# Windowed attention and a squared-ReLU MLP on one core: from the framework's order of work to an order written by a list scheduler

## The chip, the core and the metric

The kernel runs on 1 core of one Trainium2 chip. The metric is the device time of one execution in microseconds (us). The core's engines are TensorE (PE in the profile; its weight loads are PEld), VectorE (DVE), ScalarE (ACT), GpSimd (POOL) and SyncE (SP). TensorE writes its results to PSUM, 8 banks of 2 KB in each of 128 partitions, from where VectorE or ScalarE copy them to SBUF. DMAs are issued from SyncE's queue (by hardware descriptors) or GpSimd's (by software descriptors, which can also cast on the way).

## The reference

For 4 batches of 8 heads, 768 tokens, head size 64: attention in which a query sees the last 128 keys and the first 4 ("sinks"). Its output, 3072 tokens of 512, goes through two layers with a squared ReLU between them.

```python
scores = scale * np.matmul(q, k.transpose(0, 1, 3, 2))
keep = (pos[None, :] < 4) | ((rel >= 0) & (rel < 128))     # rel = query - key
a = softmax(np.where(keep, scores, -1e9))
x = np.matmul(a, v)                 # then heads side by side: (3072, 512)
h = x @ w_in                        # (512, 2048)
r = np.maximum(h, 0.0)
return (r * r) @ w_out              # (2048, 512), float32
```

Inputs and output are float32.

## The kernel before

All matmuls are in bf16. Work is tiled by 128 tokens (6 tiles, NT, to a batch) and by pairs of heads (4, NP, to a batch).

*Loads* (`load_qk_dma` line 112, `load_v` line 140, `load_w_in_dma` line 89, `load_w_out_dma` line 94): all from GpSimd's queue, cast from float32 to bf16 on the way. A head of q, k or v is one DMA of 768 rows of 64 elements. w_in is four DMAs, w_out four.

*Transposes* (`load_qk_compute`, line 124): for each head pair and each of q and k six 128x128 TensorE transposes into one PSUM tile (line 131), and one VectorE copy to `qkT` (line 138), in which the two heads of a pair lie on partitions 0 to 63 and 64 to 127.

*Attention* (line 150), head pair by head pair: scores of 64-row matmuls into two one-bank PSUM buffers (lines 171, 178), keys on the partitions, each block of 128 keys against the 256 queries that can see it; exp on ScalarE (line 185). The sinks are taken as a whole first key block of 128 against queries 256 to 767 (line 191), and a bias of -100 in the exponential (line 197) clears the rows beyond the fourth. A mask multiply on VectorE (line 203), then 15 matmuls per head with v, which carries a column of ones, so that column 64 is the softmax sum (line 224, one PSUM buffer); a reciprocal and a multiply on VectorE (lines 232, 233) write `xn`.

*Bridge* (line 240): for each token tile four transposes and a copy to `xT_sb`.

*Layer 1* (`moe1`, line 258): for each of 16 blocks of 128 hidden columns, 4 matmuls on 512 tokens and 4 on 256 (line 265), into two one-bank PSUM buffers; ReLU on ScalarE (line 272) and the square in place on VectorE (line 273). *Layer 2* (`moe2`, line 275): for each token tile 16 matmuls of 512 columns (line 281), a copy on VectorE (line 288), and the store from SyncE (line 289).

The order: the calls at the end of the kernel (lines 291 to 324) give attention of batches 0 and 1, then layer 1 and 2 of a batch followed by attention of the next but one. The framework's own scheduler reorders the instructions of these calls by readiness and priority within the buffer counts of the pools (lines 45 to 58); in the trace layer 1 of one batch runs mixed with attention of the next.

## Time and profile before

| | |
|---|---|
| time, median of 3 runs | 288.06 us (287.36 to 288.46) |
| span of the profiled execution, first to last instruction | 285.6 us |
| TensorE busy | 256.0 us, 90% |
| VectorE, ScalarE, GpSimd busy | 133.0, 125.3, 89.8 us |
| granted TensorE clock, mean | 0.998 |
| DMA packets | 81429, of which 77952 on GpSimd's software queue |

Times are microseconds, unless a column says ns. In a time table by stage each row is a stretch of the span, with the busy time of each engine and its number of instructions in brackets, then the granted clock, the DMA engines' busy share and GB/s. In the chain of waits and the timeline a row has start, length and what ran. In a list of groups a row has line, engine, operation, output and input tile with shapes, count, then busy us, mean ns of one, and the idle time before them with what ended it. In the list of DMA queues a row has packets, MB, and the packets' time as a share of 16 engines' span. A matmul's length holds its latency; matmuls overlap, so a burst is shorter than the sum of its parts.

### The profile page before, as it was taken

Reading aid. Unit: us, or ns where it says so; the run is one execution under the profiler, and the core shown is the slowest. Engines: PE = TensorE matmul, PEld = TensorE weight load, DVE = VectorE, ACT = ScalarE, POOL = GpSimd, SP = SyncE. Lnnn points to the kernel's source line nnn. Section 1 sums busy time; section 2 is a strip of 40 time slices with the busy share of each in tenths; the row PEclk is TensorE's granted clock in tenths of the full one; section 3 lists DMA queues with packets and bytes.
Section 4 is the critical chain, followed back from the end, with each engine's and each line's share of the span. In section 5 each row is a group of like instructions: output and inputs, shape, how many; then the busy total and the mean of one; then the engine's idle time right before and its main releaser. Section 6 shows DMA issues by size and latency. Waiting matters only on the chain.

```text
span 285.6 us, 4652 instructions
## 1 busy us (share of the span) xinstructions
PE 256.0 (90%) x1859; PEld 135.5 (47%) x1888; DVE 133.0 (47%) x307; ACT 125.3 (44%) x257; POOL 89.8 (31%) x127
## 2 busy tenths in 40 slices
PE   1586775999999999999999999999999999999994
PEld 0333444564555444555555445644554444555441
DVE  2343554587674212785863114776753113333211
ACT  1175540489945100798754001899553003455000
POOL 8999679775996000970000000000000000000000
PEclk9999999999999999999999999999999999999999
DMA  8979999999999012990000111000000221000121
GB/s 57 120 52 163 210 158 127 145 157 170 126 109 110 37 73 76 135 122 3 2 1 2 73 73 73 3 2 0 2 0 0 85 85 52 2 1 0 73 76 73
DMA packets 81429, 20.23 MB, mean 71 GB/s; under 512 B 75776, under 2 KB 77824, under 8 KB 81408
## 3 DMA queue, kind: packets, MB, share of 16 engines
q0 software_dynamic: 77952, 13.64, 61.1%
q1 hardware_dynamic: 3456, 6.29, 6.0%
q8 instruction: 15, 0.25, 0.4%
q14 instruction: 6, 0.05, 0.1%
HBM read 27.26 MB, written 6.29 MB: 117 GB/s over the span
## 4 chain that ended last, share of the span: by engine, by line
PE 74%; ACT 8%; DVE 6%; POOL 6%; issue 2%; DMA 2%; POOLq 0%
PE pm L281 28%; PE pm L265 27%; PE po L224 6%; POOL qn L117 5%; ACT expm L185 4%; PE ps L171 4%; PE pxt L246 3%; ACT gT L272 3%; DVE expm L203 3%; PE pt L131 2%; PE ps L191 2%; DMA v_aug<-in_v_dram 2%; PE ps L178 2%; DVE qkT L138 1%; DVE xn L233 1%
## 5 line engine op out<-in xcount | busy, mean ns | idle before, releaser
L272 ACT ACTIVATE gT<-pm 128x512 bf16<-128x512 f32 (+1 forms) x128 | 59.1, 490 | 109.2 <-PE pm L265 108.5
L265 PE MATMUL pm<-xT_sb,w_in_sb 128*128 128x256 bf16 (+1 forms) x498 | 102.6, 326 | 3.6 <-ACT gT L272 1.7
L281 PE MATMUL pm<-w_out_sb,gT 128*128 128x512 bf16 x369 | 85.2, 379 | 0.4
L265 PEld LDWEIGHTS <-w_in_sb 128*128 128x128 bf16 x512 | 46.0, 98 | 40.1 <-issue 19.7
L185 ACT ACTIVATE expm<-ps 128x512 bf16<-128x512 f32 (+1 forms) x96 | 50.1, 565 | 23.2 <-PE ps L178 22.3
L273 DVE TENSOR_TENSOR gT<-gT 128x512 bf16<-128x512 bf16 (+1 forms) x128 | 42.4, 353 | 38.0 <-ACT gT L272 37.4
L281 PEld LDWEIGHTS <-gT 128*128 128x128 bf16 x384 | 37.5, 98 | 41.4 <-DVE gT L273 0.6
L288 DVE COPY osb<-pm 128x512 f32<-128x512 f32 x24 | 16.6, 692 | 59.1 <-PE pm L281 59.1
L117 POOL DMA_DIRECT2D qn<-in_q_dram x32 | 27.1, 867 | 26.3 <-PE pt L131 23.3
L203 DVE TENSOR_TENSOR expm<-expm,mask_B 128x1408 bf16<-128x1408 bf16 x32 | 27.7, 886 | 7.6 <-ACT expm L185 5.7
L117 POOL DMA_DIRECT2D qn<-in_k_dram x32 | 27.0, 870 | 7.3 <-DMA w_in_sb<-in_moe_w_in_dram 2.7
L131 PE MATMUL pt<-ident,qn 128*128 128x128 bf16 x192 | 18.6, 243 | 10.4 <-DMA qn<-in_q_dram 6.9
L171 PE MATMUL ps<-qkT 64*128 64x256 bf16 x96 | 23.1, 301 | 4.5 <-ACT expm L185 2.6
L145 POOL DMA_DIRECT2D v_aug<-in_v_dram x32 | 26.3, 873 | 2.6 <-DMA w_out_sb<-in_moe_w_out_dram 2.0
L224 PE MATMUL po<-v_aug,expm 128*128 128x65 bf16 x352 | 23.4, 206 | 3.1 <-DVE xn L233 1.8
L224 PEld LDWEIGHTS <-expm 128*128 128x128 bf16 x352 | 19.2, 105 | 12.9 <-issue 5.7
L138 DVE COPY qkT<-pt 128x768 bf16<-128x768 bf16 x32 | 17.8, 556 | 15.7 <-PE pt L131 15.2
L197 ACT ACTIVATE esink<-ps,sink_bias 128x512 bf16<-128x512 f32 x32 | 21.2, 687 | 6.0 <-PE ps L191 5.3
L131 PEld LDWEIGHTS <-qn 128*128 128x128 bf16 x192 | 14.8, 108 | 16.8 <-issue 10.3
L178 PE MATMUL ps<-qkT 64*128 64x256 bf16 (+1 forms) x96 | 21.0, 283 | 0.0
L233 DVE TENSOR_TENSOR xn<-po,rc 128x384 bf16<-128x384 f32 x32 | 17.8, 555 | 0.8
L224 PE MATMUL po<-v_aug,esink 128*128 128x65 bf16 x128 | 17.4, 206 | 0.0
(25 smaller groups left out, 95.0 us busy)
## 6 DMA issues: line engine op xcount, KB each, us to landing
out_dram<-osb SPq DMA_DIRECT2D x24, 256.0 KB, 2.0
qn<-in_q_dram POOLq DMA_DIRECT2D x32, 96.0 KB, 4.0
qn<-in_k_dram POOLq DMA_DIRECT2D x32, 96.0 KB, 3.8
v_aug<-in_v_dram POOLq DMA_DIRECT2D x32, 96.0 KB, 4.9
w_in_sb<-in_moe_w_in_dram POOLq DMA_DIRECT2D x4, 512.0 KB, 7.8
w_out_sb<-in_moe_w_out_dram POOLq DMA_DIRECT2D x4, 512.0 KB, 8.6
```

The lines of the kernel that those rows point to most:

```text
L117: nc.gpsimd.dma_start(out=qn[:, :, hp, :], in_=t_ap[b, 2 * m + hp].rearrange("(t p) d -> p t d", p=128),)
L131: nc.tensor.matmul(pt[:, 128 * t:128 * t + 128], lhsT=qn[:, t, :, :], rhs=ident, is_transpose=True, start=(t == 0), stop=(t == NT - 1),)
L145: nc.gpsimd.dma_start(out=v_aug[:, h, :, 0:64], in_=v[b, h].rearrange("(t p) d -> p t d", p=128),)
L171: nc.tensor.matmul(ps[:, 0:256], lhsT=kT[:, 128 * c:128 * c + 128], rhs=qT[:, 128 * c:128 * c + 256], start=True, stop=False,)
L178: nc.tensor.matmul(ps[:, 256:256 + w1], lhsT=kT[:, 128 * c:128 * c + 128], rhs=qT[:, 128 * c:128 * c + w1], start=False, stop=True,)
L185: nc.scalar.activation(out=expm[h][:, 512 * sub:512 * sub + L], in_=ps[:, 0:L], func=AF.Exp, scale=scale,)
L203: nc.vector.tensor_mul(expm[h], expm[h], mask_B)
L224: nc.tensor.matmul(po[:, 65 * t:65 * t + 65], lhsT=lhsT, rhs=rhs, start=(i_mm == 0), stop=(i_mm == n_mm - 1),)
L265: nc.tensor.matmul(pm[:, 0:cw], lhsT=w_in_sb[:, kb, 128 * fb:128 * fb + 128], rhs=xT_sb[:, kb, tok0 + c0:tok0 + c0 + cw], start=(kb == 0), ...
L272: nc.scalar.activation(out=dst, in_=pm[:, 0:cw], func=AF.Relu)
L273: nc.vector.tensor_mul(dst, dst, dst)
L281: nc.tensor.matmul(pm2, lhsT=gT[:, fb, 128 * t:128 * t + 128], rhs=w_out_sb[:, fb, :], start=(fb == 0), stop=(fb == NFB - 1),)
```

## The change

The program order is no longer the framework's. Each piece of work is an `Op` with the engines that may do it, a modelled cost on each, the ops that it comes after, and the buffers that it takes and gives back (`Slot`). `Plan.run` plays these through once while the kernel is built: of all ready ops it takes the one with the earliest modelled start, in ties the smallest key, and on the engine that would end it first; in this order the instructions are written out, and each engine and queue runs them in this order (`manual_schedule`).

Also changed:

- q, k and v are loaded from SyncE's queue as float32, a head pair to a DMA for q and k, with partition p taking n neighbouring tokens; for batch 0 the first 512 tokens and the last 256 are separate. A copy on GpSimd, VectorE or ScalarE (`regroup`, `cast`) makes bf16 of them. The copy out of the transposes (`unload`) restores the order of the tokens. w_in comes in two halves on GpSimd's queue, the first behind v's third head pair; the second part of batch 0's q and k waits for v's fourth.
- PSUM is one pool of four two-bank tiles. Scores of a head pair, half a layer-1 step (two blocks of 512 tokens, or four of 256), two token tiles of layer 2, or the transposes of q and k of a pair take one each. Exponentials, ReLU and squares run on up to 1024 columns.
- Sinks: the 4 sink keys of all 8 heads lie in one 128-column operand (`kblk`), so four accumulating matmuls and one exponential a batch give the sink scores of all heads, and `vs` holds the sink rows of v for each head.
- Masks are made from two triangles; a masking step runs on VectorE or as selects on GpSimd.
- Most SBUF tiles are allocated once: `qkT`, `xn` and `gT` single, `v`, `xT` and the sink operands double. ReLU writes a separate tile, and the square writes `gT` from it.
- Layer 2 is cut into pieces of four matmuls; attention of batch b+1 has keys that spread it over layers 1 and 2 of batch b. The last store is in two parts, the last eviction on two engines.

The core of the diff:

```diff
+LATENCY = 0.2
+PE_SLACK = 0.4
+DMA_LATENCY = 2.0
...
+            for o in ready:
+                t = o.at
+                need = {}
+                for s in o.takes:
+                    need[s.pool] = need.get(s.pool, 0) + 1
+                ok = True
+                for p, n in need.items():
+                    if len(free[p]) < n:
+                        ok = False
+                        break
+                    t = max(t, sorted(free[p])[n - 1] + LATENCY)
+                if not ok:
+                    continue
+                pick = None
+                for e, c in o.engines.items():
+                    slack = PE_SLACK if e == "pe" and t > 0 else 0.0
+                    start = max(t + slack, engine.get(e, 0.0))
+                    if pick is None or start + c < pick[1] + pick[2]:
+                        pick = (e, start, c)
+                cand = (round(pick[1], 2), o.key)
+                if best is None or cand < best[0]:
+                    best = (cand, o, pick)
+            assert best is not None, "no op can run"
+            _, o, (e, start, cost) = best
+            ready.remove(o)
...
+            o.run(e)
+            engine[e] = start + cost
+            end = start + cost
+            if o.dma:
+                queue = max(queue, end) + o.dma
+                end = queue + DMA_LATENCY
+            o.end = end
...
+                    u.at = max(a.end for a in u.after) + LATENCY
...
+    sizes = dict(bank=4, qr=10, qs=6, vf=4, expm=8, r=3, osb=2)
...
+    kblk = [consts.tile([128, NP * 136], BF16, name=f"kblk{i}") for i in range(2)]
+    vs_sb = [consts.tile([128, H, D + 1], BF16, name=f"vs{i}") for i in range(2)]
+    es_sb = [consts.tile([128, 512], BF16, name=f"es{i}") for i in range(2)]
+    vs_in = consts.tile([32, B, D + 1], BF16)
+    qkT_sb = consts.tile([128, NP, 2, S], BF16)
+    v_sb = [consts.tile([128, H, NT, D + 1], BF16, name=f"v{i}") for i in range(2)]
+    xn_sb = consts.tile([128, NT, DM], BF16)
+    xT_sb = [consts.tile([128, NKB, S], BF16, name=f"xT{i}") for i in range(2)]
+    gT_sb = consts.tile([128, NFB, S], BF16)
...
+    def after_dma(dma, other):
+        tc.add_manual_dep(
+            dma.ins, other.ins.name,
+            mybir.DependencyInfo(mybir.DependencyClass.Sync, mybir.DependencyReason.DATA),
+            reason="behind the other load",
+        )
...
+    def load_w_in(half, behind):
+        def run(e):
+            c = slice(half * (DFF // 2), (half + 1) * (DFF // 2))
+            d = nc.gpsimd.dma_start(out=w_in_sb[:, :, c],
+                                    in_=moe_w_in[:, c].rearrange("(a p) f -> p a f", p=128))
+            if behind is not None:
+                after_dma(d, loaded[behind])
+            loaded["w_in", half] = d
+        w_in_op[half] = op(-0.9 + 0.01 * half, {"pool": 0.6}, run, dma=5.5,
+                           after=[ops[behind]] if behind is not None else ())
...
+    GROUPS = {b: [(0, 6)] for b in range(B)}
+    GROUPS[0] = [(0, 4), (512, 2)]
...
+            t = qr_t[b, m, ti, g] = work["qr"].tile([128, 2, n * D], FP32, name="qr", tag="qr")
+            d = nc.sync.dma_start(
+                out=t,
+                in_=(q, k)[ti][b, 2 * m:2 * m + 2, t0:t0 + 128 * n, :].rearrange(
+                    "h (p t) d -> p h (t d)", t=n))
+            if behind is not None:
+                after_dma(d, loaded[behind])
...
+                for ti in (1, 0):
+                    sl = qs_slot[b, m, ti, g] = Slot("qs", 1)
+                    def regroup(e, m=m, ti=ti):
+                        t = qs_t[b, m, ti, g] = work["qs"].tile([128, n, 2, D], BF16, name="qs", tag="qs")
+                        copy(e, t, qr_t.pop((b, m, ti, g)).rearrange("p h (t d) -> p t h d", d=D))
+                    regs.append(op(at(f), {"pool": 0.1 + n * 0.17, "dve": 0.08 + n * 0.135, "act": 0.2 + n * 0.107}, regroup,
+                                   after=[ops["qk", b, m, ti, g]] + prev_tr, takes=[sl],
...
+                                is_transpose=True, start=(t == 0), stop=(t == n - 1))
...
+                    def unload(e, m=m, ti=ti):
+                        pt = bank_t[b, m, g]
+                        copy(e,
+                             qkT_sb[:, m, ti, t0:last].rearrange("c (p t) -> c p t", t=n),
+                             pt[:, ti, 0:128 * n].rearrange("c (t p) -> c p t", t=n))
...
+            def sink_scores(e):
+                ps = bank_t["sink", b] = bank("pk", [128, 512], FP32)
+                for m in range(NP):
+                    nc.tensor.matmul(ps[:, 0:last - lo], lhsT=kb[:, 128 * m:128 * m + 128],
+                                     rhs=qkT_sb[:, m, 0, lo:last],
+                                     start=(m == 0), stop=(m == NP - 1))
...
+                    def scores(e, s=s, m0=m0):
+                        for m in (m0, m0 + 1):
+                            ps = bank_t["s", b, s, m] = bank("ps", [128, 2, 512], FP32)
+                            segs = [] if s == 0 else [(0, 2 * s - 1, 2 * s, 128)]
+                            segs += [(128, 2 * s, 2 * s, 256), (384, 2 * s + 1, 2 * s + 1, 128)]
+                            for i, (o, c, qb, w) in enumerate(segs):
+                                for h2 in range(2):
+                                    r = slice(64 * h2, 64 * h2 + 64)
+                                    nc.tensor.matmul(
+                                        ps[:, h2, o:o + w],
+                                        lhsT=qkT_sb[r, m, 1, 128 * c:128 * c + 128],
+                                        rhs=qkT_sb[r, m, 0, 128 * qb:128 * qb + w],
+                                        start=(i == 0), stop=(i == len(segs) - 1))
...
+                            nc.scalar.activation(out=x[:, :, o:512], in_=bank_t["s", b, s, m][:, :, o:512],
+                                                 func=AF.Exp, scale=scale)
...
+                        masked.append(op(at(fm + 0.03), {"pool": 1.5, "dve": 0.8} if s else {"dve": 0.6},
+                                         domask, after=[ex, c_masks]))
...
+                    va = op(at(fm + 0.16), {"pe": 0.75 if s else 0.37}, values, takes=[bo], reads=exs,
+                            after=masked + [ops["cast", b, m, gg] for m in (m0, m0 + 1) for gg in range(g + 1)]
+                            + ([A["es", gg] for gg in range(g + 1)] if s else []) + [A["sink_operands"]] + prev_bridge)
...
+                ops["bridge", b, s] = op(at(fs + 0.36), {"pe": 0.46}, bridge, after=norms + older_layer1, takes=[bx])
...
+        a = op(key, {"pe": n * NKB * cw / 2380.0}, mm, takes=[bs],
+               after=[ops["xT", b, s] for s in need] + [w_in_op[fbs[-1] * 2 // NFB]])
...
+            nc.scalar.activation(out=r, in_=bank_t.pop(tag), func=AF.Relu)
...
+        ops["sq", b, fbs[0], c0] = op(key, {"dve": 0.7}, square, reads=[rs],
+                                      after=[ra] + [ops[x] for x in ops if x[0] == "layer2" and x[1] == b - 1])
...
+            a = op(keys(i, part), {"pe": 0.865}, mm, after=last + need + [w_out_op[part]],
+                   takes=[bs] if n == 0 else ())
...
+                if i == 0:
+                    copy("dve", o[:, 0, :], y[:, 0, :])
+                    nc.sync.dma_start(out=out[128 * g:128 * g + 128, :], in_=o[:, 0, :])
+                else:
+                    copy("dve", o[:, 1, 0:256], y[:, 1, 0:256])
+                    copy("act", o[:, 1, 256:512], y[:, 1, 256:512])
+                    nc.sync.dma_start(out=out[128 * g + 128:128 * g + 256, :], in_=o[:, 1, :])
...
+    first, rest = 0, 1
+    for m in range(NP):
+        for ti in (1, 0):
+            load_qk(-3 + 0.01 * m, 0, m, ti, first)
+    for m in range(NP):
+        load_v(-2 + 0.01 * m, 0, m, first)
+    load_w_in(0, ("v", 0, 2, first))
+    load_w_in(1, None)
+    for m in range(NP):
+        for ti in (1, 0):
+            load_qk(-1.5 + 0.01 * m, 0, m, ti, rest, behind=("v", 0, 3, first) if m == 0 else None)
+    for m in range(NP):
+        load_v(-1.4 + 0.01 * m, 0, m, rest)
+    for i in range(4):
+        load_w_out(i)
+    LO, HI = 0.05, 0.9
     for b in range(B):
+        if b == 0:
+            at = attention(0, lambda f: f - 1.0)
+            at(0, 0.0, 1.0)
+            at(1, 0.8, 1.3)
+        for i, fb in enumerate(range(0, NFB, 2)):
+            layer1(b, b + 0.333 * i / 8, (fb, fb + 1), 0, 512, (0, 1))
+        for i, fb in enumerate(range(0, NFB, 4)):
+            layer1(b, b + 0.333 + 0.167 * i / 4, (fb, fb + 1, fb + 2, fb + 3), 512, 256, (2,))
+        if b + 1 < B:
+            base = b - 1.0 if b == 0 else b - 0.3
+            for m in range(NP):
+                for ti in (1, 0):
+                    load_qk(base + 0.01 * m, b + 1, m, ti, 0)
+            for m in range(NP):
+                load_v(base + 0.1 + 0.01 * m, b + 1, m, 0)
+            attention(b + 1, lambda f, b=b: b + LO + (HI - LO) * f)(0, 0.0, 1.0)
+        for u in range(NS):
+            if b == 0:
+                layer2(b, u, lambda i, part, u=u: 0.5 + 0.5 * (part * 6 + 2 * u + i) / 24, by_part=True)
+            else:
+                layer2(b, u, lambda i, part, u=u, b=b: b + 0.5 + 0.5 * (8 * u + 4 * i + part) / 24)
+    P.run()
```

594 lines of the change are left out of this document (338 added, 256 removed).

## The prediction

> **What bounds the kernel now.** I read the page first (busy times), then the time table by stage, then the chain of waits and the timeline inside the stages, and last the instruction groups for prices.
>
> ```profile
> span 285.6 us, 4652 instructions
> PE 256.0 (90%) x1859; PEld 135.5 (47%) x1888; DVE 133.0 (47%) x307; ACT 125.3 (44%) x257; POOL 89.8 (31%) x127
> ```
>
> TensorE is busy 90% and no other engine reaches half. But a burst of one matmul is counted with its whole latency, so 256 us is an upper bound on the matmul work. The stages show more (columns: stretch, length, busy us of PE, PEld, DVE, ACT, POOL, then clock and DMA):
>
> ```profile
> 0.00:49.85 49.85, 30.00 (x245) 16.61 (x247) 20.06 (x40) 18.92 (x33) 44.17 (x70) 1.00 1.51 127
> 49.85:93.20 43.35, 41.64 (x378) 23.91 (x384) 28.29 (x70) 30.19 (x63) 32.51 (x42) 1.00 1.72 135
> 93.20:113.39 20.19, 20.09 (x98) 9.31 (x98) 4.38 (x8) 0.47 (x2) 0.00 (x0) 1.00 0.18 66
> 237.11:264.75 27.64, 26.22 (x143) 13.89 (x144) 10.58 (x33) 13.94 (x32) 0.00 (x0) 1.00 0.03 10
> 282.00:285.60 3.60, 0.00 (x0) 0.00 (x0) 0.69 (x1) 0.00 (x0) 0.00 (x0) 0.88 0.20 73
> ```
>
> Until 49.85, where the first layer-1 matmul starts, only the attention of batch 0 runs, while GpSimd is busy 44.17 of 49.85 us, most of it issuing loads. Then come three stages of layer 1 mixed with the next batch's attention, each followed by a dense layer 2 (the first of each is shown). At the end layer 1 of the last batch stands alone (27.64), then its layer 2, then 3.60 us of eviction and store.
>
> Prices of matmuls come from the chain of waits (start, length, piece):
>
> ```profile
> 98.22 10.74 PE pm L281 x49
> 250.62 1.04 PE pm L265 x4
> 254.03 1.46 PE pm L265 x8
> 255.74 1.46 PE pm L265 x8
> 264.75 8.38 PE pm L281 x38
> ```
>
> Layer 2: 11 more matmuls took 10.74 - 8.38 = 2.36 us, so 0.2145 each; 384 of them are 82.4 us. Layer 1: four 256-wide matmuls add 1.46 - 1.04 = 0.42, so one block of 128 hidden columns (four 512-wide, four 256-wide) is 4 x 0.2145 + 0.42 = 1.28, and 64 blocks are 81.8. Together 164.2 us, which the change leaves as they are. Alone, layer 1 takes 255.74 - 254.03 = 1.71 a block: it waits 0.43, partly filled with a matmul of layer 2, for its two one-bank PSUM buffers.
>
> ```profile
> 16.07 0.80 PE L131 MATMUL pt<-ident,qn 128*128 128x128 bf16 x6 [0.24 <-DMA qn<-in_q_dram]
> 180.11 0.50 PE L131 MATMUL pt<-ident,qn 128*128 128x128 bf16 x6
> 187.49 0.23 PE L246 MATMUL pxt<-ident,xn 128*128 128x128 bf16 x1
> 185.31 0.32 PE L224 MATMUL po<-v_aug,expm 128*128 128x65 bf16 x5
> 185.75 0.19 PE L224 MATMUL po<-v_aug,esink 128*128 128x65 bf16 x1
> 183.74 0.28 PE L171 MATMUL ps<-qkT 64*128 64x256 bf16 x1
> 183.86 0.27 PE L178 MATMUL ps<-qkT 64*128 64x256 bf16 x1
> 183.91 0.27 PE L171 MATMUL ps<-qkT 64*128 64x256 bf16 x1
> 188.18 0.39 PE L265 MATMUL pm<-xT_sb,w_in_sb 128*128 128x512 bf16 x1
> 188.51 0.39 PE L191 MATMUL ps<-qkT 64*128 64x512 bf16 x1
> ```
>
> Once TensorE is warm: transposes (0.50 - 0.23) / 5 = 0.054 each; values matmuls, 15 for a head, (185.75 - 185.31) / 14 = 0.0314 each; a 256-wide score 0.12 behind one of its own head (183.74 to 183.86), 0.05 when the next head, on the other 64 rows, follows. A single layer-1 matmul next to a 64-row one takes 0.33 (188.18 to 188.51) in place of 0.2145: switching in small steps loses 0.1.
>
> Attention in before, per batch: 120 values matmuls 3.8, 72 transposes 3.9, 44 256-wide scores 2.4 to 5.3, 8 sink scores at about 0.3 2.4: 12.5 to 15.4 together. After the start, 285.6 - 49.85 - 164.2 - 3.6 - 3 x (12.5 to 15.4) leaves 22 to 30 us in which the matmul stream stands still. So the time is about 50 of start, 164 of layers, 40 of attention, 26 of gaps and 3.6 of tail.
>
> **The change, part by part.** The start is the largest term.
>
> ```profile
> q0 software_dynamic: 77952, 13.64, 61.1%
> q1 hardware_dynamic: 3456, 6.29, 6.0%
> out_dram<-osb SPq DMA_DIRECT2D x24, 256.0 KB, 2.0
> w_in_sb<-in_moe_w_in_dram POOLq DMA_DIRECT2D x4, 512.0 KB, 7.8
> 1.33 0.96 POOL L117 DMA_DIRECT2D qn<-in_q_dram  x1 [0.33 <-issue]
> 282.73 0.33 SPq L289 DMA_DIRECT2D out_dram<-osb  x1
> ```
>
> Software packets cost 0.611 x 16 x 285.6 / 77952 = 36 ns of a DMA engine each; the hardware queue's, mostly 2 KB, 0.060 x 16 x 285.6 / 3456 = 79 ns. The change loads the first 512 tokens of q and k in 2048 packets of 1 KB: between these prices 4.6 to 10.1 us over 16 engines; I take 45 ns, nearer to half a 2 KB packet, 5.8 us. The same tokens of v are 4096 packets of 256 B: at 79/8 = 10 ns 2.5 us, at 36 ns 9.2 us; I take 6. Sixteen issues on SyncE at 0.33 are 5.3 us, inside the transfers. With 1.3 us to the first issue (GpSimd's first load starts at 1.33 now) and 2.0 of latency, q and k are there at about 9, v at 15 (bounds 8 to 23).
>
> Behind that: cast, last values matmuls, division, transpose, copy. The same end of batch 0 in the chain of before:
>
> ```profile
> 39.86 0.77 DVE expm L203
> ...
> 45.74 0.60 PE pxt L246 x4
> 46.84 0.60 PE pxt L246 x4
> ```
>
> From 39.86 to 49.85 it takes 10 us, with six transpose-copy steps 1.1 apart; the change has two, so I take 6: 21 to 22. The first half of w_in waits on GpSimd's queue until v of the third head pair has landed (about 14); behind it on that queue stand the other weights and any GpSimd copy. It is 2 MB, two of before's loads, which land after 7.8 us each beside other traffic: at 16 engines and 79 ns for 2 KB about 5 us, at worst 15.6. So it lands at 19 to 30. Layer 1 starts at **25** (20 to 34) instead of 49.85.
>
> In that time TensorE has, for 512 tokens, 32 + 16 transposes, 72 values matmuls, 28 scores of 256 and 4 sink scores of 256 columns: about 8 us warm. The rows above show it cold there: six transposes took 0.80 at 16.07 and 0.50 at 180.11, although the granted clock reads 1.00 in both stretches. Twice 8 still fits between 5 and 25, so I add nothing. The Trainium skill, "TensorE: Matmul & The Clock Gate", Part 1, says that the clock is halved until about 3.4 us of sustained work, which agrees with these two rows; by it the first layer-1 matmuls would lose some 1.7 us more, an estimate from that page's figure that the sum does not hold.
>
> Constants (masks, zeroed operands, ones) are made on VectorE and GpSimd before anything has landed: nothing, and about 1 to 3 us if the first regroup is late behind them.
>
> **Layers** keep their 164.2. Relu runs on 1024 columns: (596 - 384) / 256 = 0.83 ns a column below, 1.02 us, under the 1.7 that its matmuls take, with up to four two-bank buffers, so the 0.43 wait goes.
>
> ```profile
> L272 ACT ACTIVATE gT<-pm 128x512 bf16<-128x512 f32 x64 | 38.2, 596 | 106.8 <-PE pm L265 106.8
> L272 ACT ACTIVATE gT<-pm 128x256 bf16<-128x256 f32 x64 | 24.6, 384 | 2.5 <-PE pm L265 1.8
> L273 DVE TENSOR_TENSOR gT<-gT 128x512 bf16<-128x512 bf16 x64 | 27.1, 423 | 35.5 <-ACT gT L272 35.3
> L273 DVE TENSOR_TENSOR gT<-gT 128x256 bf16<-128x256 bf16 x64 | 18.2, 284 | 2.5 <-ACT gT L272 2.1
> L203 DVE TENSOR_TENSOR expm<-expm,mask_B 128x1408 bf16<-128x1408 bf16 x32 | 27.7, 886 | 7.6 <-ACT expm L185 5.7 <-POOL mask_B L78 1.9
> L138 DVE COPY qkT<-pt 128x768 bf16<-128x768 bf16 x32 | 17.8, 556 | 15.7 <-PE pt L131 15.2
> L233 DVE TENSOR_TENSOR xn<-po,rc 128x384 bf16<-128x384 f32 x32 | 17.8, 555 | 0.8
> L70 POOL TENSOR_SCALAR_AFFINE_SELECT mask_B<-mask_B 128x256 bf16<-128x256 bf16 x5 | 2.2, 517 | 0.0
> ```
>
> **Attention**: the same transposes and values matmuls (3.9 + 3.8), scores alternating heads (2.4 to 5.3), four sink scores of 0.2145 in place of eight (0.9): 11.0 to 13.9 a batch, I take 12.0. Three and a third batches remain after the start: 40 us (37 to 46).
>
> The other engines, per batch of about 53 us. VectorE: 8 copies of L138's size, 0.56 to 0.83 since they now reorder (4.4 to 6.6); 12 masks (0.63 ns a column by L203, 7.5); 12 squares (0.54 ns by L273, 0.70 each, 8.4); 6 divisions in two pieces (about 7 by L233); bridge, eviction and sinks by the same rates 7: about 35. ScalarE: exponentials 11264 columns x 0.83 plus calls 11.5, sink 0.6, relu 12.3: about 24. New regroup and cast copies, 12 of 768 columns: no row shows one; L138 (0.56) below, L70's 2.0 ns an element (1.55) above, and as nothing like it ran on GpSimd I take the upper one, 19 us on GpSimd. All are covered by 53 us of matmuls; without that cover it is a rival below.
>
> **Gaps**: the order is now fixed on every engine, so an unready step holds all matmuls behind it. There are about 140 hand-offs to TensorE after the start. Bounds: 3 us if they are always ready (dense layer 2 shows none), 26 as before. With longer steps, four two-bank buffers and attention spread over layer 2 too, I take 0.065 each, 9 us.
>
> **Tail**: the last half row-block is evicted by two engines at once: 3.3 for 3.6.
>
> Sum: 25 + 164.2 + 40 + 9 + 3.3 = 241.5 us of span. The profiled execution's span, 285.6, lies 2.5 below the median of 288.06; with that, **244.0 us**.
>
> **Rivals.** *Weights late.* GpSimd's wait for v and the traffic of the rest of q, k, v hold w_in to about 36 us. For: before's loads land slowly under traffic (7.8 us). Against: the big packets. 11 us more: 255.
>
> *GpSimd and VectorE exclude each other.* Copies on GpSimd and two-operand work on VectorE may run only in turn: 35 + 19 = 54 a batch, just above TensorE's 53, so late squares and copies open gaps; 1 to 3 us a batch and a slower start give about 256. Against: plenty of copies can go to ScalarE (24 of 53). The Trainium skill, "SBUF — State Buffer", section Who interferes with whom, says that a VectorE instruction with two SBUF inputs contends with a GpSimd instruction that reads SBUF, the later one blocking fully; that speaks against this change, and no row here can show it, since before's GpSimd reads SBUF only in building constants.
>
> *Slower: the fixed order is wrong.* If hand-offs lag because real durations differ from the modelled ones, TensorE stands at each. From 244 to 288 are 44 us; 44 / 140 = 0.31 us beyond my 0.065 is the point from which it decides; at 0.45 in all the time is 244 - 9 + 63 = 298. For: single buffers (hidden activations, attention output, transposed q and k) tie batches together, and the trace shows 0.1 lost at mere switches. Against: 0.3 at each step is half a copy of L138's kind, while four buffers can absorb one.
>
> *Better*: layer 1 at 20, 3 us of gaps, overlapping heads: 20 + 164.2 + 37 + 3 + 3.3 + 2.5 = 230.
>
> **How the numbers follow.** The forecast has 0.58 (own range 232 to 254), weights late 0.15, exclusion 0.13, better 0.06, slower 0.08. The range 228 to 270 takes in all but the last and a tail. A difference within 0.5% (286.6 to 289.5) can't be told from none here. Faster 0.90, same 0.02, slower 0.08.
>
> **What would show it.** First layer-1 matmul near 25 (right: 20 to 30; at 36, weights late). After it, layer-1 blocks at 1.28 us with little idle before them; from there to the last matmul some 213 us. Sink activations of L197's kind gone but for a few. GpSimd copies of 768 columns at 1 to 1.6 us; much longer ones, or uneven squares, mean exclusion. Waits of TensorE summing to over 40 us after the start mean that the order is wrong, and the forecast with it.

## The result and the profile after

The changed kernel takes 265.16 us, the median of 4 runs (264.36 to 265.65), against 287.78 us (287.36 to 288.46) for the kernel before beside it: a ratio of 0.921, interval 0.9185 to 0.9234. The profiled execution took 264.97 us, its span 263.2. The forecast, 244.0, is 21.2 us too low; the range of 228 to 270 holds the time, the forecast's own range of 232 to 254 does not.

The busy times:

```profile
PE 223.0 (85%) x1913; PEld 133.1 (51%) x1940; DVE 118.9 (45%) x273; ACT 136.2 (52%) x156; POOL 33.1 (13%) x49
```

TensorE is busy 33 us less than before. Cut by stage (start of the first layer-1 matmul, end of the last matmul; columns as in the prediction's table by stage):

```profile
0.00:42.98 42.98, 13.49 (x172) 10.62 (x173) 20.73 (x66) 14.02 (x19) 12.60 (x23) 0.72 1.07 227
42.98:259.16 216.18, 209.46 (x1741) 122.51 (x1767) 97.74 (x207) 121.78 (x136) 20.47 (x26) 0.99 0.32 91
259.16:263.20 4.04, 0.00 (x0) 0.00 (x0) 0.42 (x1) 0.38 (x1) 0.00 (x0) 0.76 0.17 65
```

The middle row is close to what was forecast: TensorE is empty for only 216.18 - 209.46 = 6.7 us in it. The first row is not: layer 1 starts at 42.98, not at 25, and TensorE is busy 13.49 us of that. Inside the start:

```profile
10.00:15.00 5.00, 2.86 (x33) 1.95 (x33) 1.23 (x3) 4.74 (x8) 1.26 (x2) 1.00 1.13 202
...
20.00:25.00 5.00, 0.53 (x8) 0.15 (x4) 0.05 (x1) 2.35 (x3) 0.18 (x1) 0.50 1.22 196
25.00:30.00 5.00, 0.00 (x0) 0.00 (x0) 0.00 (x0) 0.00 (x0) 0.43 (x1) 0.50 1.23 215
...
35.00:40.00 5.00, 3.96 (x69) 3.72 (x70) 3.83 (x16) 0.69 (x2) 0.00 (x0) 0.56 1.09 230
```

From 15 to 35 us TensorE has next to nothing to do, and GpSimd, VectorE and ScalarE are nearly as empty, while the DMA engines are full. The granted clock drops to 0.50 in the idle time. The chain of waits says on what it stood (start, length, piece):

```profile
4.87 0.47 SPq L291
...
7.94 4.80 SPq L291
...
20.81 3.20 SPq L291
...
24.05 0.88 SPq L274
...
24.98 7.35 DMA qr<-in_q_dram
...
32.42 0.29 DVE qs L179
...
41.91 1.03 ACT xT L177
42.98 0.38 PE pm L521
```

SyncE issued v's eight loads of the first 512 tokens (line 291) and spent up to 4.80 us on one; the first took 0.47. The second part of q and k, next on that queue, went out only behind them, from 24.05. (It did not wait for v to land: v's last load, issued at 20.81, landed 10.6 us later. The wait that the kernel asks for between loads of one queue held back nothing here.) VectorE, which runs its instructions in the order written, stood 10.34 us for a cast of v, until 30.39; the regroup of q at 32.42 follows in its order, then masks and the sink operands, and layer 1 stands behind all that. GpSimd's timeline shows what moved in that time:

```profile
4.33 0.93 POOL L245 DMA_DIRECT2D w_in_sb<-in_moe_w_in_dram  x1
...
8.93 2.33 POOL L255 DMA_DIRECT2D w_out_sb<-in_moe_w_out_dram  x3
...
30.83 0.74 POOL L245 DMA_DIRECT2D w_in_sb<-in_moe_w_in_dram  x1 [5.39 <-DMA vf<-in_v_dram]
31.56 0.93 POOL L181 CAST v<-vf 128x512 bf16<-128x512 f32 x1
```

The second half of w_in and three quarters of w_out went first. The first half, which waits for v, is issued at 30.83, and a cast of v stands behind it. The two issues of line 245 in order (KB, us from issue to landing):

```profile
w_in_sb<-in_moe_w_in_dram POOLq DMA_DIRECT2D x1, 1024.0 KB, 11.7
```

```profile
w_in_sb<-in_moe_w_in_dram POOLq DMA_DIRECT2D x1, 1024.0 KB, 12.4
```

So the second half of w_in landed at 16.0 and the first at 43.2, after layer 1 had begun at 42.98. Layer 1 did not wait for the late half: the scheduler, whose model has the second half there earlier, begins with the hidden columns of that half, and the first weight load that waits for the other is at 51.45.

The DMA queues by stretch (packets, MB, share of 16 engines' time), first 10 to 15 us, beside w_in, then 16 to 24, beside w_out:

```profile
q0 software_dynamic: 511, 0.88, 93.9%
q1 hardware_dynamic: 511, 0.13, 19.0%
```

```profile
q0 software_dynamic: 1270, 1.25, 92.2%
q1 hardware_dynamic: 1268, 0.31, 30.0%
```

This is the cause of v's slowness in one view. 511 packets against 511, and 1270 against 1268: the weights' packets on the software queue and v's on the hardware queue took turns one for one; between 16 and 24 us the two counts are equal within a few packets in every quarter of a microsecond. Between 16 and 24 us one of v's packets took 0.300 x 128 / 1268 us = 30 ns by itself, a software packet 0.922 x 128 / 1270 us = 93 ns; in the earlier stretch, with longer rows of w_in, the software packet took 147 ns. The two overlap in part (their shares sum to over 100%), so that a pair takes 128 / 1268 us = 101 ns, little more than the longer packet. That is the pace of v's loads: 512 packets, 32 to a DMA engine, in 3.20 us are one per 100 ns.

Of the groups that answer to the prediction's prices (busy us, mean ns):

```profile
L529 ACT ACTIVATE r<-pm 128x1024 bf16<-128x1024 f32 x48 | 49.1, 1025 | 29.1 <-PE pm L521 24.7 <-DVE gT_sb L534 4.3
```

```profile
L534 DVE TENSOR_TENSOR gT_sb<-r 128x1024 bf16<-128x1024 bf16 x48 | 33.2, 691 | 43.6 <-ACT r L529 43.6
...
L179 DVE COPY qkT_sb<-pt 128x768 bf16<-128x768 bf16 x10 | 9.4, 952 | 4.7 <-PE pt L342 3.2 <-ACT qkT_sb L177 1.5
```

```profile
L181 POOL CAST qs<-qr 128x768 bf16<-128x768 f32 x10 | 10.2, 1034 | 26.4 <-PE pt L342 24.6 <-DMA qr<-in_k_dram 1.4 <-POOL expm L198 0.4
```

### The profile page after: what moved, and what is told of

Same layout as the page of the kernel before. It is cut to its first block, busy times and chain, and to the rows that moved or that the text cites. A ratio compares the mean times of both kernels' runs of the same rounds, so it can differ in the third digit from the quotient of the medians.

```text
span 263.2 us, 4650 instructions
## 1 busy us (share of the span) xinstructions
PE 223.0 (85%) x1913; PEld 133.1 (51%) x1940; DVE 118.9 (45%) x273; ACT 136.2 (52%) x156; POOL 33.1 (13%) x49
## 4 chain that ended last, share of the span: by engine, by line
PE 73%; SPq 9%; DVE 6%; ACT 6%; DMA 3%; issue 2%; DVEq 0%; ACTq 0%
PE py L554 31%; PE pm L521 29%; SPq L291 7%; PE po L470 5%; DMA qr<-in_q_dram 3%; PE ps L421 3%; ACT r L529 2%; PE pt L342 2%; PE px L498 2%; ACT expm L435 2%; SPq L274 2%; DVE xn_sb L484 1%; PE pk L391 1%; DVE expm L444 1%; DVE gT_sb L534 1%
## 5 line engine op out<-in xcount | busy, mean ns | idle before, releaser
L554 PE MATMUL py<-w_out_sb,gT_sb 128*128 128x512 bf16 x367 | 86.5, 379 | 2.5 <-DVE osb L179 0.8
L521 PE MATMUL pm<-xT,w_in_sb 128*128 128x256 bf16 (+1 forms) x504 | 86.1, 325 | 1.4 <-ACT xT L177 0.9
L529 ACT ACTIVATE r<-pm 128x1024 bf16<-128x1024 f32 x48 | 49.1, 1025 | 29.1 <-PE pm L521 24.7
L554 PEld LDWEIGHTS <-gT_sb 128*128 128x128 bf16 x384 | 35.9, 98 | 41.9 <-issue 3.8
L435 ACT ACTIVATE expm<-ps 128x1024 bf16<-128x1024 f32 (+1 forms) x48 | 42.9, 953 | 19.6 <-PE ps L421 19.3
L534 DVE TENSOR_TENSOR gT_sb<-r 128x1024 bf16<-128x1024 bf16 x48 | 33.2, 691 | 43.6 <-ACT r L529 43.6
L444 DVE TENSOR_TENSOR expm<-expm,mask 128x1024 bf16<-128x1024 bf16 (+1 forms) x41 | 26.4, 657 | 32.8 <-ACT expm L435 32.1
L421 PE MATMUL ps<-qkT_sb 64*128 64x128 bf16 (+1 forms) x256 | 16.0, 252 | 8.2 <-DVE qkT_sb L179 5.6
L470 PE MATMUL po<-v,expm 128*128 128x65 bf16 x352 | 19.8, 202 | 1.0 <-ACT expm L435 0.6
L484 DVE TENSOR_TENSOR xn_sb<-po,rc 128x256 bf16<-128x256 f32 x48 | 18.1, 419 | 0.0
L177 ACT ACTIVATE xT<-px 128x1024 bf16<-128x1024 bf16 x8 | 8.2, 1024 | 17.0 <-PE px L498 16.9
```

The costliest lines, as they stand in the source:

```text
L177: nc.scalar.activation(out=dst, in_=src, func=AF.Copy)
L421: nc.tensor.matmul(ps[:, h2, o:o + w], lhsT=qkT_sb[r, m, 1, 128 * c:128 * c + 128], rhs=qkT_sb[r, m, 0, 128 * qb:128 * qb + w], start=(i = ...
L435: nc.scalar.activation(out=x[:, :, o:512], in_=bank_t["s", b, s, m][:, :, o:512], func=AF.Exp, scale=scale)
L444: nc.vector.tensor_mul(x[:, :, o:512], x[:, :, o:512], mk[:, :, o:512])
L470: nc.tensor.matmul(pv[:, i, h2, :], lhsT=lhsT, rhs=rhs, start=(n_ == 0), stop=(n_ == len(mms) - 1))
L484: nc.vector.tensor_tensor(out=xn_sb[:, 2 * s + i, 128 * m0:128 * m0 + 256].rearrange("p (j h d) -> p j h d", j=2, d=D), in0=pv[:, i, :, :, ...
```

## The experiments

The theories. A: v's many small packets starve beside the weights, and all else follows from the order that was written for an earlier v. Its rivals: the first half of w_in, issued at 30.83, is what layer 1 waits for; or GpSimd and VectorE hold each other up. Two further questions were what keeps the gaps small, and what a repaired start is worth. Times are medians; the kernel before took 288.12, 287.87 and 287.80 us beside the three groups.

### Weights behind v's first part

```diff
-    load_w_in(1, None)
+    load_w_in(1, ("v", 0, 3, first))
...
-        load_w_out(i)
+        load_w_out(i, ("v", 0, 3, first))
```

> The second half of w_in and the four w_out loads wait, as the first half of w_in does, until v of the first 512 tokens has landed (fourth head pair). Theory A (these 6 MB of weights, issued at 4.3 to 11 us, take the DMA engines from the small packets of v, so that the 8 issues of v fill 19 us of SyncE's queue and the last cast of v comes at 31.6): the 8 issues of v take under 9 us, the last v lands at 14 to 18, the first layer-1 matmul comes at 25 to 29 in place of 43, and the time is 247 to 252 us. Theory B (v's 4096 packets of 256 B are that slow whatever runs beside them): v as late as before, first layer-1 matmul at 40 to 44, time 262 to 267.

Measured: 263.44 us, ratio 0.9146 (0.9116 to 0.9176). SyncE's timeline (start, length, count) and the chain before layer 1:

```profile
4.86 7.04 SPq L294 DMA_DIRECT2D vf<-in_v_dram  x8
...
18.39 18.80 SPq L294 DMA_DIRECT2D vf<-in_v_dram  x8
```

```profile
25.98 16.22 DMA vf<-in_v_dram
...
42.61 1.92 ACT expm L438 x2
...
45.49 0.58 PE pm L524
```

Without weights beside them v's first eight loads take 7.04 us instead of 19.14: the first half of A is shown. But layer 1 starts at 45.49, no earlier. The weights now run beside v's second part, whose eight loads take 18.80 us for half the packets, and their casts stand ahead of everything on GpSimd and ScalarE:

```profile
38.90 0.40 POOL L181 CAST v<-vf 128x256 bf16<-128x256 f32 x1 [17.08 <-DMA vf<-in_v_dram]
```

GpSimd waited 17.08 us for them. The starved piece is not the one that layer 1 needs next; it is in front of it in the order. So the time misses A's 247 to 252: A has the loads right, not what their repair is worth by itself.

### Only w_out behind v, and w_in at once

```diff
-        load_w_out(i)
+        load_w_out(i, ("v", 0, 3, first))
```

> Only the four w_out loads wait for v; the second half of w_in is still issued at 4.3 us. Theory A: a third of the early weights (2 of 6 MB) is left in the way of v, so the start lies between: first layer-1 matmul at 29 to 35, time 251 to 257. Theory B: no change, 262 to 267.

Measured: 263.47 us, 0.9157 (0.9132 to 0.9182). v's issues took 12.61 us beside the half of w_in, those of its second part 16.36, and layer 1 started at 45.67: a miss for A, in layer 1 and in time, for the reason of the first experiment.

```diff
-    load_w_in(0, ("v", 0, 2, first))
+    load_w_in(0, None)
```

> The first half of w_in is issued at 4.3 us without waiting for v; nothing else is held back. Theory C (layer 1 starts late because the first half of w_in is issued only at 30.8): layer 1 starts at 30 to 38, time 251 to 260. Theory A: v is still behind the weights, now 8 MB of them, the last values matmuls of the first 512 tokens come at 37 or later, layer 1 at 41 to 48, time 262 to 270.

Measured: 264.22 us, 0.9172 (0.9143 to 0.9201). All of w_in goes out at once, v's issues take 21.39 us, and layer 1 starts at 47.14, later than in the changed kernel. That w_in alone holds layer 1 falls, as the landings of the changed kernel say too.

### GpSimd out of the copies and masks

```diff
-                    regs.append(op(at(f), {"pool": 0.1 + n * 0.17, "dve": 0.08 + n * 0.135, "act": 0.2 + n * 0.107}, regroup,
+                    regs.append(op(at(f), {"dve": 0.08 + n * 0.135, "act": 0.2 + n * 0.107}, regroup,
...
-                                          {"pool": 0.1 + 0.17 * n, "dve": 0.08 + n * 0.135, "act": 0.2 + n * 0.107}, cast,
+                                          {"dve": 0.08 + n * 0.135, "act": 0.2 + n * 0.107}, cast,
...
-                        masked.append(op(at(fm + 0.03), {"pool": 1.5, "dve": 0.8} if s else {"dve": 0.6},
+                        masked.append(op(at(fm + 0.03), {"dve": 0.8} if s else {"dve": 0.6},
```

> Regroup and cast copies and masks may run on VectorE and ScalarE only; GpSimd keeps the constants and the weight loads. Exclusion theory (GpSimd's copies and VectorE's two-operand work hold each other up): the time falls by 2 us or more, to 263 or less, although two engines carry the work of three. Other theory (GpSimd's 27 us of copies are plain help, and VectorE and ScalarE have room at 45% and 52%): 264 to 269 us, squares at 0.69 us as before.

Measured: 263.92 us, 0.9168 (0.9148 to 0.9189). GpSimd's busy time falls from 33.1 to 9.9 us, VectorE's rises from 118.9 to 126.9, and the time is what other edits without effect give (0.9172 and 0.9178 here). It lies between the two theories' figures (263 or less, 264 or more), so neither a cost of exclusion nor a gain from GpSimd's help can be seen in the time. In single instructions something of the kind does show. VectorE's regroup copies of 768 columns in the changed kernel:

```profile
L179 DVE CAST qs<-qr 128x768 bf16<-128x768 f32 x5 | 3.4, 673 | 0.0
```

One of the five took 1173 ns while GpSimd was copying; the other four, with no GpSimd work beside them, took 541 to 553, and without GpSimd's copies the thirteen of this run take 550 in the mean. Such copies are few: with a cast of v that took 887 ns, VectorE's copies lose some 1 us in all.

### The weights' packets made shorter

```diff
-            d = nc.gpsimd.dma_start(out=w_in_sb[:, :, c],
-                                    in_=moe_w_in[:, c].rearrange("(a p) f -> p a f", p=128))
+            for c0 in range(c.start, c.stop, 256):
+                d = nc.gpsimd.dma_start(
+                    out=w_in_sb[:, :, c0:c0 + 256],
+                    in_=moe_w_in[:, c0:c0 + 256].rearrange("(a p) f -> p a f", p=128))
...
+            for c0 in (0, 256):
...
+                    out=w_out_sb[:, 4 * i:4 * i + 4, c0:c0 + 256],
```

> Nothing is held back, but the weights are loaded in DMAs of 256 columns, so that their packets are a quarter (w_in) and a half (w_out) as long. Theory A2 (packets take turns one for one): a packet of v then waits for a shorter one, 50 to 70 ns in place of 100 to 150; the 8 issues of v take 10 to 14 us in place of 19, layer 1 starts at 33 to 38, time 255 to 261 us. Rival (the DMA engines share by bytes, or v's issue on SyncE is slow in itself): issues of v as before, 17 to 21 us, time 263 to 268.

Measured: 263.31 us, 0.9145 (0.9118 to 0.9173). The weights' order is as in the changed kernel, only their rows are cut to 256 columns. SyncE's timeline and the chain:

```profile
4.87 12.99 SPq L294 DMA_DIRECT2D vf<-in_v_dram  x8
```

```profile
19.06 10.94 DMA qr<-in_q_dram
...
30.10 0.29 DVE qs L179
```

The same bytes in front of v, in shorter packets: v's issues fall from 19.14 to 12.99 us. So a small packet waits for the length of the other queue's packet, which confirms the turns by an edit. But layer 1 (41.29) and the time miss the expected 33 to 38 and 255 to 261. The second part of q, behind v on the queue, is issued at 19.06 and takes 10.94 us to land, still beside weights; VectorE regroups it at 30.10 in place of 32.42, and layer 1 stands behind that as before. Only 2.3 of the 6 us won on v's issues reach it.

### All of batch 0's q, k and v ahead of the weights

```diff
-    load_w_in(0, ("v", 0, 2, first))
-    load_w_in(1, None)
...
-            load_qk(-1.5 + 0.01 * m, 0, m, ti, rest, behind=("v", 0, 3, first) if m == 0 else None)
+            load_qk(-1.5 + 0.01 * m, 0, m, ti, rest, behind=None)
...
+    load_w_in(0, ("v", 0, 3, rest))
+    load_w_in(1, ("v", 0, 3, rest))
     for i in range(4):
-        load_w_out(i)
+        load_w_out(i, ("v", 0, 3, rest))
```

> All weights wait until all of batch 0's v, the last 256 tokens too, has landed; the second part of q and k waits for nothing. Theory A2 (packets of v and of the weights take turns one for one on the DMA engines, so whichever part of v is beside the weights comes at 100 ns a packet in place of some 25; in the run with weights behind the first part of v it was the second part, and the engines that wait for it hold layer 1): all of v lands by 20 to 24, the first half of w_in some 7 us later, layer 1 starts at 28 to 33, time 249 to 255 us. Rival (the attention chain of 512 tokens itself takes until past 40, whatever lands when): layer 1 at 40 or later, 261 us or more.

Measured: 270.30 us, 0.9392 (0.9369 to 0.9416): a miss of the expected 249 to 255, and slower than the changed kernel.

```profile
4.94 7.35 SPq L294 DMA_DIRECT2D vf<-in_v_dram  x8
...
17.57 5.18 SPq L294 DMA_DIRECT2D vf<-in_v_dram  x8
...
27.05 30.52 SPq L294 DMA_DIRECT2D vf<-in_v_dram  x6
```

```profile
45.25 14.61 DMA vf<-in_v_dram
...
66.86 2.90 PE pm L524 x11
```

Batch 0's v is issued in 7.35 and 5.18 us, as it should be. Then batch 1's v, issued from 27.05, meets the weights: six loads take 30.52 us. The scheduler's model has it there early and places its casts ahead of batch 0's remaining work, so layer 1 of batch 0 waits until 66.8 for a load that it does not need. A was right about the transfer and incomplete about the damage: this comes from the fixed order.

### A dearer v in the model

```diff
-        ops["v", b, m, g] = op(key, {"sp": 0.2}, run, takes=[sl], dma=16 * n * 0.0214,
+        ops["v", b, m, g] = op(key, {"sp": 0.2}, run, takes=[sl], dma=16 * n * 0.1,
```

with the weights behind v's first part, as in the first experiment. In this kernel the first 512 tokens of batch 1 pass on to layer 1 the attention output of the block after them, so the values differ in that part; the amount of work is the same.

> Weights behind the first part of v as in the first experiment, and the price of a v load in the scheduler's model is raised from 0.0214 to 0.1 us a packet row, what the trace shows beside weights; the loads themselves are the same. Theory A3 (the late layer 1 of the first experiment is queueing: casts of the second part of v, modelled as early, stand ahead of the copies that layer 1 needs): with the right price the order puts the first 512 tokens ahead, layer 1 starts at 27 to 32 although the second part of v lands at about 42, some of that is lost again before the last 256 tokens, time 250 to 258 us. Rival (order doesn't matter, data is late): layer 1 at 43 to 47, 262 to 266.

Measured: 256.56 us, 0.8919 (0.888 to 0.8958), 6.9 us below the first experiment, which has the same loads and the old price. SyncE's timeline and the chain:

```profile
18.27 23.74 SPq L294 DMA_DIRECT2D vf<-in_v_dram  x8
```

```profile
18.97 19.55 DMA vf<-in_v_dram
...
46.42 0.30 DVE v L179
...
47.41 1.03 ACT r L532
...
48.48 3.57 PE pm L524 x8
```

v's second part is slower still, 23.74 us of issues, yet layer 1 starts at 29.25 instead of 45.49. Only the modelled price changed: the casts now stand behind work that is ready. Later in layer 1 a cast on VectorE (46.42) still stands in front of a square; the next ReLU waits for it, and TensorE for the ReLU.

### One load at a time

Both halves of w_in behind v's first part, batch 0's remaining q, k and v behind w_in, w_out behind those, price 0.1 for batch 1's v alone; batch 1's loads, and each later batch's, behind v of the batch before.

```diff
-            load_qk(-1.5 + 0.01 * m, 0, m, ti, rest, behind=("v", 0, 3, first) if m == 0 else None)
+            load_qk(-1.5 + 0.01 * m, 0, m, ti, rest, behind=("w_in", 1))
...
-        load_v(-1.4 + 0.01 * m, 0, m, rest)
+        load_v(-1.4 + 0.01 * m, 0, m, rest, behind=("w_in", 1))
     for i in range(4):
-        load_w_out(i)
+        load_w_out(i, ("v", 0, 3, rest))
```

> The loads take turns by waits, so that nothing of batch 0's v runs beside weights: first 512 tokens of q, k, v; both halves of w_in; the last 256 tokens; then w_out beside batch 1, whose v has the raised price of 0.1 in the model; each later batch's loads wait for the batch before. Also, the handle of the bridge's PSUM tile is kept for each token block. Theory A2 with A3 (taking turns one for one, and engines queueing behind late casts): v of 512 tokens lands by 15, w_in's first half by 22, layer 1 starts at 24 to 28, the last 256 tokens are there by 35, little is lost after that, time 245 to 252 us. Rival (a later bound, such as w_out or batch 1's loads, takes up what the start gives): layer 1 at 24 to 28 but 256 us or more.

Measured: 261.22 us, 0.9065 (0.9038 to 0.9092). The chain:

```profile
25.62 3.63 PE pm L524 x16
...
32.24 3.08 DMA qr<-in_k_dram
...
35.79 3.59 DMA vf<-in_v_dram
...
43.19 16.66 DMA qr<-in_k_dram
```

Layer 1 starts at 25.62: 25 was there to be had. But batch 0's remaining k and v now arrive late (3.08 and 3.59 us in the chain), batch 1's k, issued at 43.19 beside w_out, later still (16.66), and most of the gain is gone: the start is as the theory had it, the time as its rival had it. What was left out of the first 25 us must still be moved beside something.

### Short weight packets, behind v, with a price of 0.06

```diff
-            d = nc.gpsimd.dma_start(out=w_in_sb[:, :, c],
-                                    in_=moe_w_in[:, c].rearrange("(a p) f -> p a f", p=128))
+            for c0 in range(c.start, c.stop, 256):
+                d = nc.gpsimd.dma_start(
+                    out=w_in_sb[:, :, c0:c0 + 256],
...
-        ops["v", b, m, g] = op(key, {"sp": 0.2}, run, takes=[sl], dma=16 * n * 0.0214,
+        ops["v", b, m, g] = op(key, {"sp": 0.2}, run, takes=[sl], dma=16 * n * 0.06,
...
-                    px = bank_t["x", b] = bank("px", [128, NKB, 256], BF16)
+                    px = bank_t["x", b, s] = bank("px", [128, NKB, 256], BF16)
...
-    load_w_in(1, None)
+    load_w_in(1, ("v", 0, 3, first))
```

(w_out likewise; the PSUM tile of the bridge is kept per block.)

> The short weight packets of the seventh experiment, all weights behind the first part of v as in the first, the price of v in the model at 0.06, and the bridge's PSUM handle kept for each block. Theory A2 with A3: the second part of v comes in 8 to 12 us of issue in place of 18.8 to 23.7, layer 1 starts at 27 to 32, the wait for the second part shrinks, time 249 to 256 us. Rival (short packets make the weights themselves late): layer 1 past 34, 257 us or more.

Measured: 249.71 us (247.94 to 250.07), 0.8666 (0.8633 to 0.8699): faster than both kernels, and within the expected 249 to 256. The busy times (span 247.9) and the chain:

```profile
PE 224.9 (91%) x1940; PEld 132.0 (53%) x1940; DVE 120.4 (49%) x268; ACT 137.8 (56%) x164; POOL 35.9 (14%) x57
```

```profile
14.74 8.60 DMA w_in_sb<-in_moe_w_in_dram
...
23.63 21.75 DMA w_out_sb<-in_moe_w_out_dram
```

TensorE's busy time is close to that of the changed kernel (223.0), its share 91% instead of 85%. v's second part is issued in 9.55 us, layer 1 starts at 29.30, and 218.6 us follow, against 220.2. v of batch 1 still takes 24.49 us to issue (33.81 to 58.3), but the longest wait for it is 0.51 us on GpSimd. The chain of the first 45 us now runs over the weights themselves: 8.60 for a piece of w_in, 21.75 for the second of w_out's eight loads, behind which layer 2 begins.

### The gaps: attention bunched, and three PSUM tiles

```diff
-    LO, HI = 0.05, 0.9
+    LO, HI = 0.05, 0.5
```

> Keys of the next batch's attention run from 0.05 to 0.5 of a batch in place of 0.05 to 0.9, so that it is written out beside layer 1, as the kernel before had it, and layer 2 stands alone. Theory (spreading attention over layer 2 keeps the gaps small): 3 to 9 us slower, 267 to 275. Rival (the four two-bank buffers alone close the gaps): within 2 us, 263 to 267.

Measured: 264.01 us, 0.9178 (0.9153 to 0.9202), no different from the changed kernel: spreading the attention of the next batch over layer 2 as well is not what keeps the gaps small.

```diff
-    sizes = dict(bank=4, qr=10, qs=6, vf=4, expm=8, r=3, osb=2)
+    sizes = dict(bank=3, qr=10, qs=6, vf=4, expm=8, r=3, osb=2)
...
-                layer2(b, u, lambda i, part, u=u: 0.5 + 0.5 * (part * 6 + 2 * u + i) / 24, by_part=True)
+                layer2(b, u, lambda i, part, u=u: 0.5 + 0.5 * (part * 6 + 2 * u + i) / 24, by_part=False)
```

> PSUM has three two-bank tiles in place of four, and layer 2 of batch 0 takes its token tiles one pair after another, since three pairs at once would hold all three; the rest as changed. Theory (the gaps after the start are small because four tiles let TensorE run ahead of the engines that empty them): 5 to 15 us slower, 270 to 280. Rival (the written-out order alone does it): within 3 us, 262 to 268.

(The PSUM tile of the bridge is kept per block here too.) Measured: 272.91 us, 0.9483 (0.9466 to 0.9501), span 270.7. By stage:

```profile
43.45:266.70 223.25, 211.42 (x1768) 122.16 (x1767) 100.53 (x212) 120.47 (x134) 16.98 (x22) 1.00 0.30 87
```

Layer 1 starts at 43.45, nearly as in the changed kernel; from there 227.3 us follow instead of 220.2, and TensorE is empty for 223.25 - 211.42 = 11.8 us instead of 6.7. So with three tiles the part after the start is 7 us longer, of which 5.1 are empty time of TensorE. The order of the pieces of batch 0's layer 2 was changed with it and is not told apart.

## Why the prediction came out as it did

Direction and range were right, the size was not: 22.6 us were gained where 44 were forecast, and 265.16 fits no single account of the prediction (its own 244, the rivals' 255, 256, 298 and 230); only the range drawn around them all holds it. The 21.2 us are: start +18.0, gaps +3.0, tail +0.7, time outside the span -0.7 (264.97 - 263.2 = 1.8 where 2.5 was taken), and 0.2 from the profiled execution to the median.

**Start, 25 taken, 42.98 measured: the step that failed.** It is the one that priced v at 6 us and put "v at 15 (bounds 8 to 23)". By itself v costs nearly what was said: 30 ns a packet where 6 us for 4096 packets over 16 engines are 23, and 7.04 us of issues where nothing stands beside it. Three things were wrong. First, of the waiting half of w_in it said that "behind it on that queue stand the other weights". A list scheduler issues what is ready: the second half of w_in and w_out, which wait for nothing, went in front, and the diff shows it (only half 0 has a `behind`, and the choice is by earliest modelled start). Second, with the weights thought to be behind it, v was priced as if it had the DMA engines to itself, and no term stood for two queues that are busy together. They share by packets, so a load in 256 B packets slows from 30 to 100 or 150 ns a packet, and v's casts ran until 32.5. The Trainium skill, "DMA: Bandwidth & Descriptors", section Queues, rings and completion order, says that each DMA engine goes round the queues that have work, a packet at a time; by it a packet of v waits for one of the weights' each time, and the trace agrees (1270 against 1268). The page counts several descriptors to a packet; what the profile counts as a packet alternates singly here. Third, the prediction's path gives each load the work that needs it; in the fixed order work that layer 1 doesn't need yet, such as the regroup of the second part of q, stands before it on the same engine. With the weights behind v's first part and the order left, layer 1 still started at 45.49; with the model's price of v raised as well, at 29.25.

*Attention in the start* was slower for one further reason: after idling, TensorE ran its values matmuls of 37 us at a granted clock of 0.56 (35 to 40 us): 48 took 2.58 us where 24 later take 0.74. That is an effect of the wait and not its cause.

**Layers, 164.2, and attention, 40**, hold by their unit prices: four layer-2 matmuls in a row take 0.86 us (0.215 each), twelve transposes 0.67, 24 values matmuls 0.74 (0.031 each).

**Gaps, 9 taken, 12.0 measured**: 263.2 - 42.98 - 164.2 - 40 - 4.04. TensorE is empty for 6.7 of them; the other 5.3 lie inside its busy time. These are what the unit prices leave over, not a sum of measured waits. The argument from four two-bank tiles is borne out (three cost 7.0 us more after the start, with layer 2's order changed beside it), the one from attention spread over layer 2 too was not (bunching it changed nothing). The point from which a wrong order would decide, 0.31 us more per hand-off, is far from the 12.0 / 140 = 0.09 measured.

**Tail, 3.3 taken, 4.04 measured.**

**The other engines.** ReLU on 1024 columns took 1025 ns (1.02 us forecast), a square 691 (0.70), the copies to `qkT` 952 on VectorE where 0.56 to 0.83 was taken. A GpSimd copy of 768 columns took 1034 ns, nearer to the lower bound than to the 1.55 that was taken, and GpSimd was given 33.1 us in all, not 19 a batch. Taking copies and masks from GpSimd did not move the time; the others were not varied.

**Rivals.** *Weights late* put layer 1 at 36 because w_in is held behind v. The half that is held did land late, at 43.2, but layer 1 began with the other one, and issuing all of w_in at once made it later (47.14). The cause runs the other way: the weights made v late, and v then the half of w_in that waits for it. *Exclusion* was not borne out as a cost: VectorE's squares are even (691 ns, and 690 with GpSimd out), and taking GpSimd out gains and loses nothing measurable. The Trainium skill, "SBUF — State Buffer", section Who interferes with whom, names contention between these two engines; a few of VectorE's copies here agree with it (673 ns in the mean, 550 with GpSimd out), but at a GpSimd share of 13% the time shows no cost of it. *The fixed order is wrong* fell for the body of the kernel, but its mechanism is what made the late v so dear: with the same loads the price of v in the model alone moved the time from 263.44 to 256.56 (the latter in the kernel that hands on another block's attention output; the kernel of 249.71 does not, and has a raised price as well). *Better* (230) was not reached; its start of 20 is below the 25.62 of the run that cleared the first 25 us for it.

What stays open: how the 249.71 divides between short packets and price, since shorter packets alone and waiting weights alone gain about 2 us at most, and the two were not run together without the price.

## What to carry to other kernels

When a change moves small-row loads to another queue, look at which large-row loads will be busy beside them: price the small ones at about the length of one of the others' packets each (a pair took 101 ns where the packets took 30 and 93), and ask what is ready first, not what is written first. In an order fixed by a model, a transfer that is modelled too cheap costs more than its own delay, because its consumers stand in front of work that is ready; so correct the model's price before rearranging the loads, and correct both before judging either. Behind a cured load the next late one can stand in the order, so a single repair that gains nothing doesn't clear its cause. And see which half of a split load the order uses first before blaming the half that came late.

## What the runs showed of the hardware that was not expected

- The software queue's and the hardware queue's packets go one for one: 511 to 511 and 1270 to 1268 in the changed kernel. Cutting the weights' rows to 256 columns cut v's issues beside them from 19.14 to 12.99 us.
- SyncE's issue of such a load lasts as long as its packets take to go (3.20 us beside w_out, 0.47 for the first), so that all behind it on the queue is late too. That a ring of limited length is full is an inference; no run varied it.
- The granted clock drops to 0.50 once TensorE has idled (20 to 30 us above), but in the first 12 us it reads 1.00 while TensorE runs at half its later pace. PE's timeline of the changed kernel:

```profile
6.30 1.89 PE L342 MATMUL pt<-ident,qs 128*128 128x128 bf16 x16 [6.30 <-DVE qs L179]
```

The 16 transposes, less one latency of 0.29 (a single one at 8.95), took 0.107 us each, against 0.67 / 12 = 0.056 later. At the start of a trace the durations say more of the clock than its column.
